# Nine transposed blocks instead of sixteen per attention tile, with new transfer costs in the planner of the first part

## The chip, the core and the metric

The kernel runs on one core of a Trainium2 chip. The metric is the device time of one execution in microseconds. Of the kernel before there are three timed runs (1258.95, 1251.04 and 1256.79 us, median 1256.79), and one execution with a profile.

## What is computed

Three layers follow each other. All matrices arrive in float32.

```python
# attention: 8 batches, 8 heads, 576 rows, 64 columns; keys and values are means over 8 neighbours: 72 per batch
k_p = k.reshape(B, H, Sp, pool, D).mean(axis=3)
v_p = v.reshape(B, H, Sp, pool, D).mean(axis=3)
attn = softmax(scale * q @ k_p.T)          # 576 x 72 for each head
x = attn @ v_p                             # put together to 4608 tokens x 512
# second layer, 512 -> 1024 -> 512
h = x @ w_in
ln = layernorm(h * softmax(h)) * g_ln
x = ln @ w_out
# third layer, 512 -> 2048 -> 512
h = x @ w2_in
out = (h * sigmoid(1.702 * h)) @ w2_out
```

## The kernel before, in words

Every fp32 factor is split into two fp16 parts, high and low, and a product is the sum of three fp16 products (high by high, high by low, low by high). The kernel has two parts. The **first part** computes the attention and the second layer in 36 tiles of 128 tokens, and meanwhile prepares the weights of the third layer: it joins the words of a float64 input, forms seven combinations of quarter matrices and writes their halves to DRAM. The **second part** (L1290 and the lines around it) computes the third layer in 12 blocks of 384 tokens by a Strassen-like scheme of seven products; its order is written out by hand and the change does not touch it.

In the first part a tile takes these steps. The scores go to `psx` (TensorE), the row maxima, exponentials and row sums give the normalized weights `e` (128 tokens x 8 heads x 72). ScalarE copies `e` to fp16 as the high half, VectorE or GpSimd subtracts to get the low half, and both go into `st`. A transposing DMA turns `st` into `aT`, in which the 72 keys lie on the partitions. TensorE multiplies `aT` with the transposed values `vst` into `psv`, ScalarE and VectorE split that into `xT`. Then `psh` holds x @ w_in, from which come the maximum `hmx`, the exponential `he`, the product `tt` with its sum, and the layer norm; `zs` is the fp16 split of its result, turned by another transposing DMA (16 blocks of 128x128) into `zT`. `psy` holds ln @ w_out; ScalarE copies it to `y`, and a DMA writes that to `y_dram`, from where the second part reads it. A transposed block is 128x128 fp16, which is 32 KB.

**The layout of the attention before.** A head has 256 columns in `st`: high (72), low (72), high again (72) and 40 zeros, so two blocks of 128 per head and 16 per tile. Values of a pair of heads have 256 columns in `vx` (high, high, low and 40 zeros), so eight blocks per batch in `vst`. A product of 216 used rows is so summed up by two matmuls over 128 partitions, each with 64 stationary columns (one head); the two heads of a pair write the upper and the lower 64 partitions of `psv`. Of the 36 tiles, 32 lie within one batch and four (4, 13, 22 and 31) in two, with 64 tokens of each; such a tile has twice the products, each over 64 columns.

**What sets the order.** The steps of all tiles, batches and weight chunks are generators (`attention`, `values`, `keys`, `Pair`, `Quarter`) that yield operations to a planner (`Plan`). It holds for each engine and for the DMA the time until which it is taken, picks the operation with the smallest start time (moved a little by due times), and emits it; each engine then runs its instructions strictly in that order. An operation that several engines could do (`VG`: VectorE or GpSimd) goes where it would end first. The cost of a transfer is written in `D` (L504 emits it): bytes over 360 per ns, and 1.23 times that if it transposes. All DMAs are issued by SyncE (SP) in one queue. The matmuls of the first part are emitted by `T` (L512), operations of the other engines by `op` (L475), so one line stands for many groups and the tiles' names tell them apart.

`vst` and `st` have two buffers each (by batch and by tile), `aT` two, `psv` and `psy` one, `y` two.

Of the kernel before, what the change touches and what calls it, by code (L numbers as in the profile page):

```python
# [18 lines left out]
P = 128  # L19
# [9 lines left out]
KM = DM // P  # L29
K1 = DF1 // P  # L30
K2 = DF2 // P
HS = 256
YB = 2 * P
TB = 384
TH = TB // 2
# [245 lines left out]
def moe_kernel(ctx: ExitStack, tc: tile.TileContext, qT, kT, vT, w_in, w_out, g_ln, w2_in, w2_out, eye, outT):  # L281
# [135 lines left out]
    with ExitStack() as ph:  # L417
# [9 lines left out]

        w1i = [wp.tile([P, KM, DF1], F16, name=f"w1i{i}") for i in range(2)]
        w1o = [wp.tile([P, K1, DM], F16, name=f"w1o{i}") for i in range(2)]
        vst = [wp.tile([P, H, P], F16, name=f"vst{i}") for i in range(2)]  # L430
        kbd = [wp.tile([P, NPAIR, 2 * SP], F32, name=f"kbd{i}") for i in range(2)]
        st = [wp.tile([P, H, HS], F16, name=f"st{i}") for i in range(2)]
        vx = kv.tile([P, NPAIR, 2 * P], F16, name="vx", bufs=1)

        plan = Plan()
        start, drop = plan.start, plan.drop
# [53 lines left out]
        def V(name, *args, **kw):  # L490
            return op(("dve",), name, args, kw)
# [4 lines left out]
        def VG(name, *args, **kw):  # L496
            return op(("pool", "dve"), name, args, kw)

        def A(**kw):
            return op(("act",), "activation", (), kw)  # L500

        def D(dst, src, turn=False, short=1):
            def emit(engine):
                (nc.sync.dma_start_transpose if turn else nc.sync.dma_start)(dst, src)  # L504

            n = math.prod(dst.shape) * mybir.dt.size(dst.dtype)
            return Op(("sp",), emit, [dst], [src], {"sp": n / 360 * (1.23 if turn else short)}, turn)

        def T(products):
            def emit(engine):  # L510
# [273 lines left out]
        def values(b, due):  # L784
            vp = yield from pooled("v", b, vT, due)
            am, alln, up, dn = s1("vam"), s1("v_all"), s1("v_up"), s1("v_dn")
            yield absmax_op(am, vp, axis=AX.XY)
            yield from largest(am, alln, TINY, b < 2)
            yield from power_scale("_v", alln, V_TOP, up, dn)
            yield lambda: b == 0 or v_ready[b - 1]  # L790
            yield A(
                out=vx[:, :, 0 : 2 * SP].rearrange("p a (r k) -> p a r k", r=2),
                in_=vp.unsqueeze(2).to_broadcast([P, NPAIR, 2, SP]), func=AF.Copy, scale=up,
            )
            yield V(
                "scalar_tensor_tensor", out=vx[:, :, 2 * SP : 3 * SP], in0=vp, scalar=up, in1=vx[:, :, 0:SP],
                op0=ALU.mult, op1=ALU.subtract,
            )
            drop(vp)
            yield lambda: b < 2 or valued[last_tile(b - 2)]  # L800
            yield D(vst[b % 2], vx.rearrange("p a k -> p (a k)"), turn=True)
            v_ready[b] = True
            yield w_in_done.over
            both = s1("v_sc", 2)
            c, ci = both[:, 0:1], both[:, 1:2]
            yield V("tensor_scalar", out=c, in0=dn, scalar1=1.0 / NPOOL, scalar2=w1i_dn, op0=ALU.mult, op1=ALU.mult)
            yield V("tensor_scalar", out=ci, in0=up, scalar1=w1i_up, scalar2=CI_LEAST, op0=ALU.mult, op1=ALU.max)
            yield V("tensor_scalar_min", ci, ci, CI_MOST)
            for t in range(NTILE):
                for o, n, tb in spans(t):  # L810
                    if tb == b:
                        yield G("tensor_copy", h_sc[o : o + n, t], both[o : o + n])
            h_ready[b] = True

        def attention(t):

            yield lambda: t == 0 or q_loaded[t - 1]
            qt = yield New(sb, [P, NPAIR, P], F32, "qt", bufs=2)
            q_loaded[t] = True
            yield D(qt, qT[t])  # L820
            if t < 2:
                tiles[t].due = max(due(t) + LAG_ATT, DUE_ATT + STEP_ATT * t)
            yield lambda: all(k_ready[b] for _, _, b in spans(t)) and (t == 0 or scored[t - 1])
            e = yield New(sb, [P, H, SP], F32, "e", bufs=2)
            yield there(qt, *(kbd[b % 2] for _, _, b in spans(t)))
            ps = yield New(psx, [P, 2, 512], F32, "psx", "psx")
            yield T(
                [
                    (
                        ps[o : o + n, p // 2, (p % 2) * 2 * SP : (p % 2 + 1) * 2 * SP],  # L830
                        qt[:, p, o : o + n],
                        kbd[b % 2][:, p, :],
                        True,
                        True,
                    )
                    for p in range(NPAIR)
                    for o, n, b in spans(t)
                ]
            )
            scored[t] = True  # L840
            drop(qt)
            s4 = ps[:, :, : 4 * SP].rearrange("p a (h k) -> p a h k", k=SP)
            mx = s1("mx", H)
            m3 = mx.rearrange("p (a h) -> p a h", a=2)
            yield V("tensor_reduce", out=m3, in_=s4, axis=AX.X, op=ALU.max, negate=True)
            if plan.free["act"] + ACT_SPARE < plan.free["dve"]:
                for h in range(H):
                    yield A(out=e[:, h], in_=s4[:, h // 4, h % 4], func=AF.Exp, bias=mx[:, h : h + 1])
                drop(ps)
            else:  # L850
                yield V(
                    "tensor_tensor", out=e.rearrange("p (a h) k -> p a h k", a=2), in0=s4,
                    in1=m3.unsqueeze(3).to_broadcast([P, 2, 4, SP]), op=ALU.add,
                )
                drop(ps)
                yield A(out=e, in_=e, func=AF.Exp)
            rs = s1("rs", H)
            yield V("tensor_reduce", out=rs, in_=e, axis=AX.X, op=ALU.add)
            yield A(out=rs, in_=rs, func=AF.Copy, scale=1.0 / A_TOP, bias=1e-9 / A_TOP)
            yield V("reciprocal", rs, rs)  # L860
            yield VG("tensor_tensor", out=e, in0=e, in1=rs.unsqueeze(2).to_broadcast([P, H, SP]), op=ALU.mult)
            yield lambda: t < 2 or turned[t - 2]
            s = st[t % 2]
            yield A(
                out=s[:, :, 0 : 3 * SP].rearrange("p h (r k) -> p h r k", r=3)[:, :, 0:3:2],
                in_=e.unsqueeze(2).to_broadcast([P, H, 2, SP]), func=AF.Copy,
            )
            yield VG("tensor_tensor", out=s[:, :, SP : 2 * SP], in0=e, in1=s[:, :, 0:SP], op=ALU.subtract)
            drop(e)
            aT = yield New(sb, [P, 2 * H, P], F16, "aT", bufs=2)  # L870
            yield D(aT, s.rearrange("p h c -> p (h c)"), turn=True)
            turned[t] = True
            yield lambda: all(v_ready[b] for _, _, b in spans(t)) and (t == 0 or valued[t - 1])
            yield there(aT, *(vst[b % 2] for _, _, b in spans(t)))
            ps = yield New(psv, [P, DM], F32, "psv", "psv")
            yield T(
                [
                    (
                        ps[h % 2 * D64 : (h % 2 + 1) * D64, h // 2 * P + o : h // 2 * P + o + n],
                        vst[b % 2][:, h // 2 * 2 + c, h % 2 * D64 : (h % 2 + 1) * D64],  # L880
                        aT[:, 2 * h + c, o : o + n],
                        c == 0,
                        c == 1,
                    )
                    for p in range(NPAIR)
                    for o, n, b in spans(t)
                    for c in range(2)
                    for h in (2 * p, 2 * p + 1)
                ]
            )  # L890
            valued[t] = True
            drop(aT)
            xT = yield New(sb, [P, 2 * KM, P], F16, "xT", bufs=2)
            turned_x = ps.rearrange("p (k t) -> p k t", t=P)
            yield A(out=xT[:, 0:KM], in_=turned_x, func=AF.Copy, scale=1.0 / A_TOP)
            yield V(
                "scalar_tensor_tensor", out=xT[:, KM:], in0=turned_x, scalar=1.0 / A_TOP, in1=xT[:, 0:KM],
                op0=ALU.mult, op1=ALU.subtract,
            )
            drop(ps)  # L900
            x_turned[t] = xT
# [269 lines left out]
        def clear(i, on):  # L1171
            if i == 0:
                yield G("memset", ones, 1.0)
                yield G("memset", minus_half, -0.5)
            yield on("memset", kbd[i], 0.0)
            yield on("memset", st[i], 0.0)
            if i == 0:
                yield G("memset", vx[:, :, 3 * SP :], 0.0)

        def eye_load():  # L1180
            yield D(eye_t, eye)
# [298 lines left out]
```

## Time and profile before

| | |
|---|---|
| median of three runs | 1256.79 us (1251.04 to 1258.95) |
| the profiled execution | 1253.29 us, of which the span from first to last instruction is 1251.5 us |
| TensorE busy | 1143.5 us, 91% |
| ScalarE, VectorE, GpSimd busy | 766.5, 730.9 and 664.7 us |
| DMA | 152.85 MB, of which the 16 engines moved most in the first 500 us |
| mean granted TensorE clock | 0.986 of full speed |

The first part ends at about 539 us, when the last product of `psy` is done; the second part takes the rest, with TensorE busy nearly throughout. A number such as 128x512 behind an operation is partitions by elements. The release named at an idle time ("<-DVE xT") is the event that came last before the instruction began.

### The profile page before, as it was taken

Reading aid. Unit: us, or ns where it says so; the run is one execution under the profiler, and the core shown is the slowest. Engines: PE = TensorE matmul, PEld = TensorE weight load, DVE = VectorE, ACT = ScalarE, POOL = GpSimd, SP = SyncE. Lnnn points to the kernel's source line nnn. Section 1 sums busy time; section 2 is a strip of 40 time slices with the busy share of each in tenths; the row PEclk is TensorE's granted clock in tenths of the full one; section 3 lists DMA queues with packets and bytes.
Section 4 is the critical chain, followed back from the end, with each engine's and each line's share of the span. In section 5 each row is a group of like instructions: output and inputs, shape, how many; then the busy total and the mean of one; then the engine's idle time right before and its main releaser. Section 6 shows DMA issues by size and latency. Waiting matters only on the chain.

```text
span 1251.5 us, 27586 instructions
## 1 busy us (share of the span) xinstructions
PE 1143.5 (91%) x11678; PEld 989.6 (79%) x11678; DVE 730.9 (58%) x1153; ACT 766.5 (61%) x1073; POOL 664.7 (53%) x696
## 2 busy tenths in 40 slices
PE   2778998899999999889999999999999999999998
PEld 2335665576666666789999999999999898999998
DVE  7898877587677843136455454637272737364543
ACT  6998998788789855345445353627263536454552
POOL 5887998687879953424333352525262515243331
PEclk9989999899999999999999999999999999999999
DMA  9979999999989698470101010100011010101000
GB/s 324 302 205 240 269 270 256 248 231 248 256 206 234 164 230 236 109 270 8 46 14 39 14 40 20 33 27 27 27 33 46 7 46 8 46 7 46 14 14 26
DMA packets 246524, 152.85 MB, mean 122 GB/s; under 512 B 163584, under 2 KB 226176, under 8 KB 244096
## 3 DMA queue, kind: packets, MB, share of 16 engines
q1 hardware_dynamic: 246400, 151.09, 45.5%
q8 instruction: 91, 1.49, 0.5%
q14 instruction: 33, 0.27, 0.1%
HBM read 77.66 MB, written 33.55 MB: 89 GB/s over the span
## 4 chain that ended last, share of the span: by engine, by line
PE 30%; POOL 12%; DVE 8%; ACT 8%; issue 5%; DMA 0%; ACTq 0%; POOLq 0%
PE bank_a L1290 18%; PE bank_d L1290 8%; ACT w_g L1325 6%; DVE g L1337 5%; POOL w_g L336 3%; PE bank_b L1290 3%; POOL w_g L335 3%; POOL w_g L333 2%; POOL w_g L334 2%; PE psy L512 2%; ACT g L1334 1%; DVE c L1303 1%; POOL zs L475 1%; DVE w_g L333 0%; ACT c L1300 0%
## 5 line engine op out<-in xcount | busy, mean ns | idle before, releaser
L1290 PEld LDWEIGHTS <-w2i 128*128 128x128 f16 x4032 | 337.4, 98 | 34.3 <-issue 33.7
L1290 PEld LDWEIGHTS <-w2o 128*128 128x128 f16 x4032 | 335.0, 98 | 7.4 <-issue 6.8
L333 POOL TENSOR_TENSOR w_g<-w_g 128x384 f32<-128x384 f32 x36 | 43.6, 1211 | 379.3 <-ACT w_g L1325 379.3
L1290 PE MATMUL bank_a<-ys,w2i 128*128 128x192 f16 x2304 | 215.1, 247 | 27.1 <-ACT c L1300 25.0
L512 PE MATMUL psh<-w1i,xT 128*128 128x512 f16 x864 | 205.8, 389 | 8.9 <-DVE mean L475 8.2
L1290 PE MATMUL bank_a<-g,w2o 128*128 128x192 f16 x2304 | 206.0, 246 | 1.0
L512 PE MATMUL psy<-zT,w1o 128*128 128x256 f16 x1728 | 196.8, 273 | 8.8 <-ACT y L475 8.8
L512 PEld LDWEIGHTS <-w1o 128*128 128x128 f16 x1728 | 167.9, 98 | 35.8 <-issue 10.3
L1337 DVE SCALAR_TENSOR_TENSOR g<-w_g,gu_b,g 128x1152 f16<-128x1152 f32 (+1 forms) x96 | 169.1, 1782 | 24.5 <-ACT g L1334 24.4
L512 PEld LDWEIGHTS <-xT 128*128 128x128 f16 x864 | 84.4, 100 | 103.9 <-issue 13.8
L1300 ACT ACTIVATE c<-bank_a 128x384 f32<-128x384 f32 x192 | 91.7, 484 | 116.4 <-PE bank_a L1290 113.1
L1334 ACT ACTIVATE g<-w_g,gu_b 128x1152 f16<-128x1152 f32 (+1 forms) x96 | 132.9, 1408 | 39.4 <-POOL w_g L336 39.0
L1303 DVE SCALAR_TENSOR_TENSOR c<-bank_d,c 128x384 f32<-128x384 f32 x96 | 53.3, 555 | 134.4 <-ACT c L1300 99.5
L475 POOL TENSOR_TENSOR zs<-tt,zs 128x1024 f16<-128x1024 f32 x36 | 77.4, 2149 | 59.7 <-ACT zs L475 59.5
L1290 PE MATMUL bank_d<-ys,w2i 128*128 128x192 f16 x1152 | 107.5, 249 | 0.3 <-DVE c L1303 0.3
L1290 PE MATMUL bank_d<-g,w2o 128*128 128x192 f16 x1152 | 102.4, 246 | 3.0 <-DVE g L1337 3.0
L1325 ACT ACTIVATE w_g<-c,ch_b 128x1536 f32<-128x1536 f32 x48 | 75.3, 1568 | 36.8 <-DVE c L1303 36.7
L1300 ACT ACTIVATE c<-bank_a,co_b 128x384 f32<-128x384 f32 x47 | 26.9, 573 | 108.6 <-PE bank_a L1290 108.6
L512 PE MATMUL psx<-kbd,qt 128*128 128x144 f32 (+1 forms) x320 | 46.3, 306 | 24.6 <-ACT raw_z L475 12.7
L512 PEld LDWEIGHTS psx<-kbd,qt 128*128 128x128 f32 (+1 forms) x320 | 41.4, 193 | 29.4 <-issue 12.7
L475 POOL TENSOR_TENSOR lo<-w_f,hi 128x512 f16<-128x512 f32 (+1 forms) x46 | 62.2, 1365 | 2.7 <-ACT hi L475 2.3
L475 DVE TENSOR_REDUCE hmx<-psh 128x1 f32<-128x1024 f32 x36 | 43.7, 1214 | 34.1 <-PE psh L512 34.1
(189 smaller groups left out, 1693.1 us busy)
## 6 DMA issues: line engine op xcount, KB each, us to landing
raw<-w_out SPq DMA_DIRECT2D x12, 1024.0 KB, 6.9
raw<-w_in SPq DMA_DIRECT2D x10, 1024.0 KB, 8.0
half<-kT SPq DMA_DIRECT2D x16, 576.0 KB, 5.4
half<-vT SPq DMA_DIRECT2D x16, 576.0 KB, 5.5
qt<-qT SPq DMA_DIRECT2D x36, 256.0 KB, 3.9
y_dram<-y SPq DMA_DIRECT2D x36, 256.0 KB, 2.8
y<-y_dram SPq DMA_DIRECT2D x48, 192.0 KB, 3.2
outT<-c SPq DMA_DIRECT2D x48, 192.0 KB, 1.9
```

The source lines that it names most:

```text
L333: eng.tensor_tensor(out=w[:, 1], in0=q[:, Q12], in1=q[:, Q11], op=ALU.subtract)
L334: eng.tensor_tensor(out=w[:, 2], in0=q[:, Q22], in1=w[:, 1], op=ALU.subtract)
L335: eng.tensor_tensor(out=w[:, 0], in0=q[:, Q22], in1=q[:, Q12], op=ALU.subtract)
L336: eng.tensor_tensor(out=w[:, 3], in0=q[:, Q21], in1=w[:, 2], op=ALU.subtract)
L475: getattr(eng, name)(*args, **kw)
L512: nc.tensor.matmul(*p[:3], start=p[3], stop=p[4])
L1290: nc.tensor.matmul(bank[:, q], self.weight(p, q, kk, w), self.data(p, kk, i), start=(first and q == 0 and kk == 0 and w == 0 and i == 0), ...
L1300: nc.scalar.activation(out=self.c[:, i], in_=bank, func=AF.Copy, scale=self.scale)
L1303: nc.vector.scalar_tensor_tensor(out=self.c[:, i], in0=bank, scalar=self.scale, in1=self.c[:, i], op0=ALU.mult, op1=ALU.add)
L1325: nc.scalar.activation(out=self.w[:, 0:4], in_=self.c, func=AF.Gelu_apprx_sigmoid, scale=self.ch)
L1334: nc.scalar.activation(out=self.g[:, 0, s], in_=self.w[:, s], func=AF.Copy, scale=self.gu)
L1337: nc.vector.scalar_tensor_tensor(out=self.g[:, 1, s], in0=self.w[:, s], scalar=self.gu, in1=self.g[:, 0, s], op0=ALU.mult, op1=ALU.subtract,)
```

## The change

The layout of the attention is packed tighter, and the planner's costs of transfers are changed.

- In `st` a head has one block of 128: its 72 high columns and the low columns of its first 56 keys. The low columns of the other 16 keys of all eight heads together are a ninth block. The second copy of the high half is gone, so ScalarE writes 576 elements per token and not 1152; the subtraction becomes two, of 8x56 and 8x16 elements.
- `vx` has three blocks per pair of heads (12 per batch, not 8): high values of all keys and again of the first 56, low values of the 72 keys, and high values of the last 16 keys of both heads for the ninth block. ScalarE writes it in four operations and not one.
- A pair of heads now takes five products per part of a tile: two over the first block and two over the second, each with 64 stationary columns, as before, and one over the ninth block with 128 stationary columns for both heads.
- The zeros in `st` are no longer needed, so its two memsets go; `vx` is cleared once as a whole.
- The planner's cost of a transfer is now bytes over 330 per ns, and over 170 if it transposes (before: 360, and 360/1.23 = 293). All of its decisions from then on may differ.

```diff
+LEFT = 2 * SP - P
...
-        vst = [wp.tile([P, H, P], F16, name=f"vst{i}") for i in range(2)]
+        vst = [wp.tile([P, 3 * NPAIR, P], F16, name=f"vst{i}") for i in range(2)]
...
-        st = [wp.tile([P, H, HS], F16, name=f"st{i}") for i in range(2)]
-        vx = kv.tile([P, NPAIR, 2 * P], F16, name="vx", bufs=1)
+        st = [wp.tile([P, H + 1, P], F16, name=f"st{i}") for i in range(2)]
+        vx = kv.tile([P, NPAIR * (3 * P + 2 * LEFT)], F16, name="vx", bufs=1)
+        vx3 = vx[:, 0 : 3 * NPAIR * P].rearrange("p (g k) -> p g k", k=P)
...
-            return Op(("sp",), emit, [dst], [src], {"sp": n / 360 * (1.23 if turn else short)}, turn)
+            return Op(("sp",), emit, [dst], [src], {"sp": n / (170 if turn else 330)}, turn)
...
-            yield A(
-                out=vx[:, :, 0 : 2 * SP].rearrange("p a (r k) -> p a r k", r=2),
-                in_=vp.unsqueeze(2).to_broadcast([P, NPAIR, 2, SP]), func=AF.Copy, scale=up,
+            even, odd = vx3[:, 0::3], vx3[:, 1::3]
+            yield A(out=even[:, :, 0:SP], in_=vp, func=AF.Copy, scale=up)
+            yield V(
+                "scalar_tensor_tensor", out=odd[:, :, 0:SP], in0=vp, scalar=up, in1=even[:, :, 0:SP], op0=ALU.mult,
+                op1=ALU.subtract,
             )
...
+            yield A(out=even[:, :, SP:P], in_=vp[:, :, 0 : P - SP], func=AF.Copy, scale=up)
+            for j in range(2):
+                r = slice(j * D64, (j + 1) * D64)
+                yield A(
+                    out=vx[r].rearrange("p (a x) -> p a x", a=NPAIR)[:, :, 2 * P + j * LEFT : 2 * P + (j + 1) * LEFT],
+                    in_=vp[r, :, P - SP :], func=AF.Copy, scale=up[r],
+                )
...
+        def of_pair(out, p, at, aT, vst):
...
+            heads = [(slice(j * D64, (j + 1) * D64), 2 * p + j) for j in range(2)]
+            return [
+                *((out[r], vst[:, 3 * p, r], aT[:, h, at], True, False) for r, h in heads),
+                *((out[r], vst[:, 3 * p + 1, r], aT[:, h, at], False, False) for r, h in heads),
+                (out, vst[:, 3 * p + 2], aT[:, H, at], False, True),
+            ]
...
-            yield A(
-                out=s[:, :, 0 : 3 * SP].rearrange("p h (r k) -> p h r k", r=3)[:, :, 0:3:2],
-                in_=e.unsqueeze(2).to_broadcast([P, H, 2, SP]), func=AF.Copy,
+            first, rest = slice(0, P - SP), slice(P - SP, SP)
+            yield A(out=s[:, 0:H, 0:SP], in_=e, func=AF.Copy)
+            yield VG("tensor_tensor", out=s[:, 0:H, SP:P], in0=e[:, :, first], in1=s[:, 0:H, first], op=ALU.subtract)
+            yield VG(
+                "tensor_tensor", out=s[:, H].rearrange("p (h k) -> p h k", k=LEFT), in0=e[:, :, rest],
+                in1=s[:, 0:H, rest], op=ALU.subtract,
             )
-            yield VG("tensor_tensor", out=s[:, :, SP : 2 * SP], in0=e, in1=s[:, :, 0:SP], op=ALU.subtract)
...
-            aT = yield New(sb, [P, 2 * H, P], F16, "aT", bufs=2)
+            aT = yield New(sb, [P, H + 1, P], F16, "aT", bufs=2)
...
-            yield on("memset", st[i], 0.0)
             if i == 0:
-                yield G("memset", vx[:, :, 3 * SP :], 0.0)
+                yield G("memset", vx, 0.0)
```

TensorE's queue gains the fifth product of each pair and part of a tile, 160 in all (640 products into `psv` become 800): 128 of them over 128 moving columns, 32 (of the four tiles that lie in two batches) over 64.

The first place where rows move is ScalarE's queue at the values of batch 5. Before, `vx` is written by one instruction (`vp` are the pooled values, `v_up` their scale):

```order
L475 ACTIVATE diag_3696<-eye_t_87,vam_3266 128x128
L475 ACTIVATE tt_3411<-tt_3411,mean_2769,a_3442 128x1024
L475 ACTIVATE raw_2494<-raw_2494,w2o_up_77 128x512
L475 ACTIVATE vx_125<-vp_3037,v_up_3268 128x4x144
L475 ACTIVATE zs_3715<-tt_3411 128x1024
L475 ACTIVATE raw_2494<-raw_2494,w2o_up_77 128x512
```

With the change the four pieces have other work between them:

```order
L478 ACTIVATE tt_3241<-tt_3241,mean_2855,a_3584 128x1024
L478 ACTIVATE vx_125<-vp_3182,v_up_3447 128x4x72
L478 ACTIVATE zs_3826<-tt_3241 128x1024
L478 ACTIVATE vx_125<-vp_3182,v_up_3447 128x4x56
L478 ACTIVATE diag_3807<-eye_t_87,w2a1_144 128x128
L478 ACTIVATE vx_125<-vp_3182,v_up_3447 64x4x16 x2
```

The last write of `vx`, on which the transpose into `vst` waits, now stands behind a `zs` and a `diag` that lie between the pieces.

The second place is SP's queue at the key halves of batch 6 (`half<-kT`; tile 27 is the first that needs them). Before, both are issued behind the transposes `aT` of the first 20 tiles:

```order
L504 DMA y_dram1_64<-y_2830 128x2x256
L504 DMA_TRANSPOSE aT_2860<-st1_124 128x16x128
L504 DMA w2i_dram_69<-hi_2707 128x7x256
L504 DMA half_2946<-kT 128x1152
L504 DMA half_2947<-kT 128x1152
L504 DMA w2i_dram_69<-lo_2723 128x7x256
L504 DMA y_dram1_64<-y_2938 128x2x256
```

With the change the two stand behind the transposes of 25 tiles, apart from each other:

```order
L507 DMA_TRANSPOSE zT_3813<-zs_3826 128x16x128
L507 DMA_TRANSPOSE aT_4013<-st0_123 128x9x128
L507 DMA half_3387<-kT 128x1152
L507 DMA_TRANSPOSE zT_3813<-zs_3957 128x16x128
L507 DMA y_dram2_65<-y_3934 128x2x256
L507 DMA half_3881<-vT 128x1152
L507 DMA half_3414<-kT 128x1152
```

The key halves moved from seven tiles ahead of their use to two.

The third place is SP's queue near the end of the first part, where the weights of the second part (`w2i`) and its first tokens (`y_6097`, in the change `y_6429`) are loaded. Before:

```order
L504 DMA w2i3_5791<-w2i_dram_69 128x4096
L504 DMA_TRANSPOSE zT_6014<-zs_6016 128x16x128
L504 DMA w2i6_5794<-w2i_dram_69 128x4096
L504 DMA y_6097<-y_dram0_63 128x2x192
L504 DMA_TRANSPOSE zT_6014<-zs_6056 128x16x128
L504 DMA y_6097<-y_dram0_63 128x2x192 x3
L504 DMA y_dram4_67<-y_6135 128x2x256
L504 DMA y_dram4_67<-y_6212 128x2x256
```

And with the change:

```order
L507 DMA_TRANSPOSE zT_6245<-zs_6278 128x16x128
L507 DMA y_dram4_67<-y_6351 128x2x256
L507 DMA w2i3_6039<-w2i_dram_69 128x4096
L507 DMA w2i6_6042<-w2i_dram_69 128x4096
L507 DMA y_dram4_67<-y_6424 128x2x256
L507 DMA y_6429<-y_dram0_63 128x2x192 x3
L507 DMA_TRANSPOSE zT_6453<-zs_6455 128x16x128
```

One write of `y` now goes out ahead of the last two weight loads, and the next one ahead of the token loads.

## Rows read from the trace of the kernel before

**Rows 1.** Stretches: length, PE, PEld, DVE, ACT, POOL busy, clock, DMA share, GB/s.

```profile
36.00:95.00 59.00, 43.81 (x295) 21.97 (x294) 51.80 (x101) 54.07 (x93) 49.18 (x55) 0.88 0.90 250
95.00:450.00 355.00, 328.50 (x2638) 226.32 (x2635) 268.05 (x498) 303.37 (x479) 303.15 (x380) 0.99 0.98 235
450.00:540.00 90.00, 80.38 (x652) 61.86 (x651) 21.97 (x39) 38.96 (x50) 30.44 (x47) 1.00 0.69 188
540.00:1251.00 711.00, 680.17 (x8053) 669.81 (x8050) 360.00 (x466) 343.58 (x406) 260.86 (x188) 0.99 0.11 37
```

**Rows 2.** DMA of 95 to 450 us: queue share; issues, times, us to landing.

```profile
q1 hardware_dynamic: 171209, 83.04, 97.6%
...
aT<-st SPq DMA_TRANSPOSE x29, 4.2
zT<-zs SPq DMA_TRANSPOSE x28, 5.1
vst<-vx SPq DMA_TRANSPOSE x6, 3.4
```

**Rows 3.** Two short stretches, columns as above.

```profile
475.00:480.00 5.00, 5.00 (x29) 2.74 (x28) 3.15 (x7) 4.00 (x5) 1.86 (x2) 1.00 1.01 388
500.00:505.00 5.00, 1.98 (x19) 1.62 (x17) 1.39 (x3) 3.34 (x6) 4.60 (x8) 1.00 0.93 210
```

**Rows 4.** PE's waits, 0 to 95 us: us in total, times, longest.

```profile
PE psv L512 <- DMA aT<-st: 12.9, 4, 7.3
```

**Rows 5.** PE's waits, 95 to 500 us.

```profile
PE psv L512 <- DVE xT L475: 10.3, 5, 5.2
...
PE psv L512 <- DMA vst<-vx: 3.5, 2, 1.8
```

**Rows 6.** DVE's waits, 95 to 500 us.

```profile
DVE w2am L475 <- DMA raw<-w_out: 13.2, 4, 5.6
```

**Rows 7.** Timeline around 242 us, DVE and PE: start, us, operation, [idle before].

```profile
242.67 1.35 DVE L475 TENSOR_REDUCE kp<-half 128x144 f32<-128x1152 f32 x1 [5.77 <-DMA half<-kT]
...
245.81 0.80 PE L512 MATMUL psv<-diag,ones 128*128 128x128 f32 x2 [5.21 <-DVE xT L475]
246.40 4.50 PE L512 MATMUL psh<-w1i,xT 128*128 128x512 f16 x12
```

**Rows 8.** Timeline of PE, three groups of products in a row.

```profile
112.08 2.78 PE L512 MATMUL psy<-zT,w1o 128*128 128x256 f16 x24
114.80 0.64 PE L512 MATMUL psv<-aT,vst 128*64 128x128 f16 x16
115.37 2.79 PE L512 MATMUL psy<-zT,w1o 128*128 128x256 f16 x24
```

**Rows 9.** Groups by line: xcount, busy us, mean ns, idle before.

```profile
L512 PEld LDWEIGHTS <-w1o 128*128 128x128 f16 x1728 | 167.9, 98 | 35.8 <-issue 10.3
```

**Rows 10.** Groups of the other engines, 0 to 520 us.

```profile
L475 POOL TENSOR_TENSOR w_f<-w_f 128x256 f32<-128x256 f32 x61 | 45.9, 764 | 1.7 <-DVE w_f L475 1.0
L475 POOL TENSOR_TENSOR st<-e,st 128x576 f16<-128x576 f32 x34 | 44.7, 1315 | 10.5 <-ACT st L475 6.4 <-issue 3.6
...
L475 ACT ACTIVATE st<-e 128x1152 f16<-128x1152 f32 x36 | 41.5, 1156 | 12.2 <-POOL e L475 6.8 <-DVE e L475 5.3
...
L475 ACT ACTIVATE e<-e 128x576 f32<-128x576 f32 x36 | 24.2, 672 | 2.0 <-DVE e L475 2.0
```

**Rows 11.** Timeline near the end of the first part: SP, then ACT.

```profile
482.31 5.89 SPq L504 DMA_TRANSPOSE zT<-zs  x1
488.25 1.61 SPq L504 DMA_DIRECT2D y<-y_dram  x3
489.95 5.19 SPq L504 DMA_DIRECT2D y_dram<-y  x2
...
494.16 0.60 ACT L475 ACTIVATE y<-psy 128x512 f32<-128x512 f32 x1 [8.77 <-DMA y_dram<-y]
```

**Rows 12.** PE's waits, 500 to 545 us.

```profile
PE psy L512 <- ACT y L475: 5.3, 3, 3.0
```

More of the change, by code (lines that the diff above doesn't have):

```diff
@@ L31 @@
 K2 = DF2 // P
-HS = 256
+LEFT = 2 * SP - P
 YB = 2 * P
@@ L500, in A, with D @@
             return op(("act",), "activation", (), kw)
-        def D(dst, src, turn=False, short=1):
+        def D(dst, src, turn=False):
             def emit(engine):
@@ L790, in values @@
             yield lambda: b == 0 or v_ready[b - 1]
-            yield A(
-                out=vx[:, :, 0 : 2 * SP].rearrange("p a (r k) -> p a r k", r=2),
-                in_=vp.unsqueeze(2).to_broadcast([P, NPAIR, 2, SP]), func=AF.Copy, scale=up,
-            )
[L795 to L798, printed above, removed]
+            even, odd = vx3[:, 0::3], vx3[:, 1::3]
[3 more added lines that the diff above has]
+                op1=ALU.subtract,
+            )
+            yield A(out=even[:, :, SP:P], in_=vp[:, :, 0 : P - SP], func=AF.Copy, scale=up)
[5 more added lines that the diff above has]
+                )
             drop(vp)
             yield lambda: b < 2 or valued[last_tile(b - 2)]
-            yield D(vst[b % 2], vx.rearrange("p a k -> p (a k)"), turn=True)
+            yield D(vst[b % 2], vx[:, 0 : 3 * NPAIR * P], turn=True)
             v_ready[b] = True
@@ L877, in attention @@
                 [
[L878 to L884, printed above, removed]
+                    x
                     for p in range(NPAIR)
                     for o, n, b in spans(t)
-                    for c in range(2)
-                    for h in (2 * p, 2 * p + 1)
+                    for x in of_pair(ps[:, p * P + o : p * P + o + n], p, slice(o, o + n), aT, vst[b % 2])
                 ]
```

## The prediction

> **What bounds the kernel now.** I read the stretches first, because the shares of the whole span mix two parts with different limits. Each row of [rows 1] is a stretch with the busy time of each engine, the granted clock and the DMA's share. The reader is to see three things. From 540 us on TensorE is busy 680 of 711 us, the DMA 0.11: the second part is TensorE's, and nothing of the change lies there. From 95 to 450 us TensorE is busy 328.5 of 355 us (93%) and the DMA 0.98 of the time: two resources are nearly full at once, and TensorE's idle time of 26.5 us is the most that this stretch could give back if the work stayed as it is. From 36 to 95 us TensorE is idle 15 of 59 us at a mean clock of 0.88, while ScalarE (54) and VectorE (52) are nearly full. The tail, 450 to 540 us, has 9.6 us of idle TensorE.
>
> Next come the waits, which say what TensorE's idle time hangs on: in the first 95 us 12.9 us in four waits for `aT` [rows 4]; from 95 to 500 us 10.3 us for `xT` of VectorE and 3.5 us for `vst` [rows 5]. VectorE in turn waits for loads (13.2 us for the raw weights alone [rows 6]). The timeline shows how such a wait reaches TensorE: VectorE stands 5.77 us before `kp`, since the key halves are not there; `xT`, which is queued behind it, comes late; TensorE stands 5.21 us and then needs 4.50 us for twelve products of `psh` [rows 7], which is 375 ns for 512 columns, where two products of 256 columns in a row take 2 x 113 ns (24 in the 2.72 us from 112.08 to 114.80 [rows 8]). That is its lower clock level after the pause.
>
> **The change, part by part.** The sum is made against the profiled execution's own 1253.3 us, which is 3.5 us under the median of the three runs and inside their spread.
>
> *Products (+8.3).* 128 more over 128 columns and 32 over 64. The trace has no fp16 product of 128 stationary and 128 moving columns. From below: 113 ns for 256 columns, so 57 for 128 and 28 for 64 [rows 8], in all 8.2 us. From above: a load of 128 weight columns takes 98 ns [rows 9]; if none of it were hidden, 160 x 98 = 15.7 us. I take the row that is nearest in shape: 16 half-width products of `psv` last from 114.80 to 115.37, so a pair of them, which fills the array's width once, takes 71 ns [rows 8]; 128 x 71 + 32 x 36 = 10.3 us. 29 of 36 tiles lie behind 95 us [rows 2], where TensorE is nearly full: 8.3 us on the path (6.6 to 12.6). The other seven tiles lie in the stretch with 15 us of idle time and cost nothing unless that goes.
>
> The Trainium skill (TensorE: Matmul & The Clock Gate, section Back-to-back issue gap) gives about 81 ns for a product of 128 columns in a sustained stream with weight loads, and only 56 for one by itself; by it, as an estimate, the products would cost some 11.7 us and not 10.3, and the sum would be a little over 1 us higher. No row here shows such a stream.
>
> *Transposed blocks.* In the stretch 95 to 450 us, `aT` has 29 x 16 blocks, `zT` 28 x 16 and `vst` 6 x 8: 960 blocks of 32 KB, or 31.5 of the 83.0 MB [rows 2]. The cheapest price is that of two `zT` nearly alone: 0.93 of 5 us for 1.05 MB, 0.145 us per block, or 226 GB/s [rows 3]. The dearest comes from the whole stretch: plain loads at 388 GB/s and share 1.01 [rows 3] would need 134 us for the other 51.6 MB; 346 us are used, which leaves 212 us for 960 blocks, 0.22 each. The change takes away 29 x 7 blocks and adds 6 x 4: 179 fewer, so 26 to 39 us of 346, and the DMA's share falls to some 0.88. This is not a term of the sum: it pays only through waits.
>
> The Trainium skill (Advanced Engine Details and Errata, section X-Bar Transpose (TRN2)) says that transposes run as fast as plain transfers, at 350 to 400 GB/s. The trace disagrees: 226 GB/s in the stretch where little else runs [rows 3]. By the page the blocks would save only about 15 to 17 us (an estimate), the planner's new price would be false, and the next two gains would be about half of what I take.
>
> *Waits of the first 95 us (-4).* A transposition of nine blocks is shorter by seven, 1.0 to 1.5 us; four waits [rows 4] give 4 to 6 us. I take the low end, because the chain before it (GpSimd's subtraction) gets no shorter. Bounds: 0, and the whole 12.9.
>
> *VectorE's waits for loads (-9).* The stall of [rows 7] costs 5.2 us and about 1.8 us by the lower clock (4.50 against 12 x 0.226 = 2.7). Its key halves were issued and read early; in the new order they are issued five tiles later, alone, and VectorE's read is moved back too. With the DMA no longer full I take that 7.0 as gone, and 2 of the other 5.1 us of waits for `xT` [rows 5]. Late next is `hmx`, which waits for TensorE and so costs nothing. Bounds: the whole 10.3 + 1.8, and a new wait of the same size (+7), as the halves now have two tiles to spare and not seven.
>
> *The values at a change of batch (+5).* `vst` gets 12 blocks for 8: 0.6 to 0.9 us longer. ScalarE writes `vx` in four pieces: two rows give it 0.84 ns per element and 188 ns fixed (1152 in 1156 ns, 576 in 672 [rows 10]), so 0.43 + 0.38 + 2 x 0.24 = 1.29 us where one instruction of 576 elements took about 0.67; and between the pieces stand a `zs` (1024 elements, about 1.05 us) and a `diag` (0.30). `vst` comes some 2.5 us later than now, six times behind 95 us. Two of these were waited for already [rows 5]: 2 x 2.5 = 5. Bounds: 0 where products of other tiles cover it, 15 if all six are bare.
>
> *The tail (-4).* ScalarE's `y` stood 8.77 us for the write of an earlier `y`, which was issued only at 489.95, behind a `zT` and three token loads [rows 11]; behind it on ScalarE are the next `zs`, and TensorE then waited 5.3 us for `y` [rows 12]. The new order issues these writes ahead of the last weight loads and the token loads. I take 4 of the 5.3. Bounds: 0, -9.6.
>
> *Off the path.* ScalarE saves 36 x 0.48 = 17 us on `st` and gives back 8 x 0.6 on `vx`; it is busy 303 of 355 us and does not end the waits. GpSimd has two subtractions (448 and 128 elements) for one of 576: by 1315 and 764 ns for 576 and 256 elements [rows 10] one more fixed part of about 0.32 us, 31 times, 10 us in all. TensorE covers it while GpSimd is at 303 of 355 us [rows 1]; without that cover it would cost the share behind 95 us, 8 us. The memsets at the start go or shrink; TensorE has no work then, and VectorE's is under 1 us.
>
> Sum: 8.3 - 4 - 9 + 5 - 4 = -3.7, so 1249.6 us. **I forecast 1250 us**, no change by measure. A change of under 1% (12.6 us: under 1244.2 or over 1269.4 against the median) can't be told from none here.
>
> **The rivals.**
> - *The forecast*, gains and costs nearly cancel: 1243 to 1257, chance 0.42; a third of it lies under 1244.2.
> - *The DMA was the bound*, and TensorE's idle time falls to 2% of the stretch: (328.5 + 8.3) / 0.98 = 344 for 355, -11; with the head and the tail, 1234. For it: share 0.98, and VectorE's waits for loads. Against: the second part, with the DMA at 0.11, still has TensorE idle for 4% [rows 1], and at that the stretch would need 352. Chance 0.18.
> - *The freed DMA time buys nothing*: the waits stay and only change places, since the order is another one throughout; then +8.3 for the products and up to +5 for the values, 1258 to 1267. This is also the case that the new prices don't do what they say: at 170 GB/s the planner holds back transfers that by [rows 3] can run at 226. Chance 0.26.
> - *Slower*: the full-width product cannot overlap its weight load with the half-width ones around it, and each costs the 98 ns of [rows 9], 12.6 us behind 95 us; with the values' 5 and no gain this is 1271, and more with bare batch changes. It decides from about 85 ns per product on, narrow ones too (160 x 0.085 x 29/36 = 11, and 5, so +16 against the profiled execution). For it: TensorE is 93% full where they come. Against: `psv` took 71 ns per pair with two loads in it. The skill's 81 ns lies just under that point. Chance 0.14.
>
> **The numbers.** Faster: 0.18 + 0.14 = 0.32. Slower: 0.14 and a rest of the third case, 0.15. Within 1%: 0.53. The range leaves out the deep end of the second case and the slower one: 1232 to 1268.
>
> **What will show it.** Products: the gap from one group's start to the next around 20 products of `psv`; 0.85 us (0.57 + 4 x 0.071) if right, 0.96 if at 98 ns. Blocks: the DMA's share over the same stretch at 0.86 to 0.90. Waits: PE's waits for `aT` in the first 95 us near 9, none of 5 us behind `kp`, `vst` waits near 8, `y` waits after 500 us under 2. I am wrong if the last `psy` ends before 525 or after 552 us, for the second part should last its 711 us in any case.

## The result: 1% slower, by a product that I priced more than three times too low

The change takes 1267.03 us (median of 8 runs, 1263.54 to 1272.15), the kernel before 1257.55 us over as many runs. The ratio is 1.0104 (95% interval 1.0081 to 1.0127), 9.5 us by the medians. The range ended at 1268, so the time lies inside it; the direction and the forecast of 1250 are wrong. The profiled execution of the change is the slowest of its runs, 1272.15 us with a span of 1270.4; that of the kernel before (1253.29) lies under its median. The two traces are so 18.9 us apart, twice the 9.5 us of the medians, and lengths taken from them overstate the loss.

The stretches of the profile after, as in [rows 1] (length; PE, PEld, DVE, ACT, POOL busy; clock; DMA share; GB/s):

```profile
36.00:95.00 59.00, 46.31 (x295) 24.39 (x294) 49.30 (x96) 50.24 (x93) 49.46 (x60) 0.94 0.78 223
95.00:450.00 355.00, 342.33 (x2619) 231.07 (x2621) 266.45 (x488) 282.45 (x483) 289.89 (x383) 0.97 0.87 212
...
557.00:1270.00 713.00, 681.07 (x8062) 670.79 (x8061) 361.74 (x467) 343.90 (x407) 261.09 (x188) 0.99 0.11 37
```

The last products of `psy`, before and after (timelines of PE: start, us, operation, number):

```profile
530.25 5.40 PE L512 MATMUL psy<-zT,w1o 128*128 128x256 f16 x48 [0.73 <-ACT y L475]
...
548.83 5.40 PE L515 MATMUL psy<-zT,w1o 128*128 128x256 f16 x48 [0.19 <-ACT y L478]
```

They end at 535.7 and 554.2 us, the latter past the 552 that I had named as a sign of being wrong. Then follows a wait of 3.4 us in both, and the second part lasts 713 us as before (711). The DMA share fell from 0.98 to 0.87, as forecast (0.86 to 0.90). TensorE is busier than before, 342 of 355 us for 328.5, and yet the stretch contains fewer products of `psy` and `psh` (1152 and 612 for 1228 and 642), since the first part lasts longer. So TensorE was not kept waiting; it had more to do. The granted clock of the stretch is 0.97 for 0.99. The timeline of PE around one group of `psv` (start, us, operation, number):

```profile
453.61 2.78 PE L515 MATMUL psy<-zT,w1o 128*128 128x256 f16 x24
456.32 1.65 PE L515 MATMUL psv<-aT,vst 128*64 128x128 f16 x20
457.80 2.78 PE L515 MATMUL psy<-zT,w1o 128*128 128x256 f16 x24
```

From the start of the group to the start of the next it is 1.48 us (1.49 in most others); before, it was 0.57 for 16 products [rows 8]. I had named 0.85 as right and 0.96 as the sign of the slower rival; it is neither. A tile that lies in two batches takes 2.44 us (443.43 to 445.87) for 0.62 before (419.65 to 420.27). Over the first part that is 32 x 0.92 + 4 x 1.82 = 36.7 us more work for TensorE, where I had 10.3.

The waits of PE, as in [rows 4, 5, 12] (us in total, times, longest), first 0 to 95, then 95 to 500, then 500 to 570 us:

```profile
PE psv L515 <- DMA aT<-st: 1.9, 2, 1.5
...
PE psv L515 <- DVE xT L478: 1.7, 2, 1.3
...
PE psy L515 <- DMA zT<-zs: 2.6, 2, 2.0
PE psy L515 <- ACT y L478: 1.3, 2, 1.1
```

`aT` is waited for 1.9 us and not 12.9, `xT` 1.7 and not 10.3, `y` 1.3 and not 5.3; `vst` is not in the list. The forecast signs of a gain are there, and the kernel is slower.

### The profile page after: what moved, and what is told of

It is laid out like the page before. It is cut to its first block, busy times and chain, and to the rows that moved or that the text cites. A ratio compares the mean times of both kernels' runs of the same rounds, so it can differ in the third digit from the quotient of the medians.

```text
span 1270.4 us, 27958 instructions
## 1 busy us (share of the span) xinstructions
PE 1183.9 (93%) x11838; PEld 1010.2 (80%) x11838; DVE 739.3 (58%) x1154; ACT 757.4 (60%) x1104; POOL 673.5 (53%) x728
## 4 chain that ended last, share of the span: by engine, by line
PE 54%; POOL 15%; DVE 13%; ACT 10%; issue 5%; DMA 3%; SPq 0%; ACTq 0%; DVEq 0%; POOLq 0%
PE bank_a L1302 18%; PE psh L515 11%; PE psy L515 10%; PE bank_d L1302 8%; ACT w_g L1337 6%; DVE g L1349 5%; PE psv L515 4%; POOL w_g L336 3%; POOL w_g L335 3%; PE bank_b L1302 2%; POOL w_g L333 2%; POOL w_g L334 2%; PE psx L515 2%; POOL w_f L478 1%; ACT g L1346 1%
## 5 line engine op out<-in xcount | busy, mean ns | idle before, releaser
L515 PE MATMUL psh<-w1i,xT 128*128 128x512 f16 x864 | 209.3, 393 | 10.3 <-DVE mean L478 4.0
L515 PEld LDWEIGHTS <-vst 128*64 128x64 f16 (+1 forms) x800 | 39.2, 107 | 40.2 <-issue 16.7
L515 PE MATMUL psv<-aT,vst 128*64 128x128 f16 (+3 forms) x800 | 65.5, 232 | 5.4 <-DMA aT<-st 3.0
```

Source lines behind the costliest of these rows:

```text
L515: nc.tensor.matmul(*p[:3], start=p[3], stop=p[4])
```

## Experiments

Each kernel ran interleaved with the kernel before, whose median was 1254.4 to 1256.0 us in these runs.

**1 and 2. Which products cost the time.** Both keep the change's order on every engine and alter only the products of `psv`: e1_halves does the wide one (128 stationary columns) as two of 64, e2_grouped puts all 64-column products of a tile (the first four of each pair) ahead of its four wide ones.

```diff
 e1_halves, in of_pair
-                (out, vst[:, 3 * p + 2], aT[:, H, at], False, True),
+                *((out[r], vst[:, 3 * p + 2, r], aT[:, H, at], False, True) for r, h in heads),
```

> The ninth block's product is done as two products with 64 stationary columns (one head each) and not as one with 128; the order of every engine is otherwise that of the change. Theory (each change between 64 and 128 stationary columns on TensorE costs time: in the trace of the change a pair of heads takes 0.37 us where two pairs of half-width products took 0.142): a pair now takes 3 x 0.071 = 0.21 us, a tile's group 0.85 us and not 1.49, TensorE has some 26 us less work, and the time falls to 1241 to 1252 us. Rival 1 (a third set of products per pair is dear in itself, by its number): the group stays at 1.2 us or more, 1260 or more. Rival 2 (the new order of the planner made it slower, and TensorE's products lie beside other waits): 1262 to 1272 whatever the group takes.

```diff
 e2_grouped, in attention
-            yield T(
...
+            products = [
+                x
+                for part in (slice(0, 4), slice(4, 5))
+                for p in range(NPAIR)
+                for o, n, b in spans(t)
+                for x in of_pair(ps[:, p * P + o : p * P + o + n], p, slice(o, o + n), aT, vst[b % 2])[part]
+            ]
+            yield T([(*x[:3], i < 2, i == len(products) - 1) for i, x in enumerate(products)])
```

> The same products as in the change, but within a tile all 64-column ones come first and the four 128-column ones last, so that a tile has two changes of width and not eight. Theory (the change of width costs): a group takes about 0.57 + 4 x 0.057 + one or two changes of 0.09 = 0.9 to 1.0 us and not 1.49; 1244 to 1254 us. Rival 1 (a 128-column product over 128 moving columns takes 0.23 us by itself, as its weight load is not hidden): the group stays at 1.4 to 1.5 us and the time at 1264 to 1271. Rival 2 (the order): 1262 to 1272 whatever the group takes.

e1_halves: 1247.14 us, ratio 0.993 (0.9901 to 0.9958). e2_grouped: 1246.22 us, 0.9926 (0.9905 to 0.9947). The timelines of PE, first e1_halves:

```profile
454.49 0.86 PE L515 MATMUL psv<-aT,vst 128*64 128x128 f16 x24
455.28 2.79 PE L515 MATMUL psy<-zT,w1o 128*128 128x256 f16 x24
```

and e2_grouped, the last line from the timeline of the weight loads (PEld):

```profile
455.82 0.97 PE L515 MATMUL psv<-aT,vst 128*64 128x128 f16 x20
456.63 2.78 PE L515 MATMUL psy<-zT,w1o 128*128 128x256 f16 x24
...
456.57 0.10 PEld L515 LDWEIGHTS <-w1o 128*128 128x128 f16 x1
```

The load of the next weights, those of `psy`, starts 0.06 us ahead of its product, while wide products of `psv` still run. 24 half-width products take 0.79 us, and the very products of the change, sorted by width, 0.81 us. So a product with 128 stationary columns costs (0.81 - 0.57) / 4 = 60 ns, near the 57 of my lower bound and under the 81 ns that I had quoted from the Trainium skill (TensorE: Matmul & The Clock Gate, Back-to-back issue gap). Both times hold one change of width, away from the half-width products. It is the change of width between neighbours that costs: rival 1 of each expectation falls by its own run, rival 2 by both. Sorting also moves a wide product away from the half-width ones that sum into the same columns of `psv`; e7 tells the two apart. The time fell by 20 us where I had expected 13 to 26.

**7. The mix of widths in the old kernel.** To see it without nine blocks and without a new order, the kernel before got one more product of 128 stationary columns per pair and part of a tile, times a tile of zeros (`zero`); the planner does not count it, so the order stays. The line that adds it:

```diff
+                ] + [(ps[:, p * P + o : p * P + o + n], vst[b % 2][:, 2 * p], zero[:, o : o + n], False, True)]
```

> The kernel before, its order and its 16 blocks, with one more product per pair and part of a tile: 128 stationary columns of vst times a tile of zeros, added to the same psv, so that the values do not change. It puts the change's mix of widths into the old kernel and nothing else. Theory (width changes cost): a tile's group takes about 1.5 us and not 0.57, TensorE has 37 us more work, of which waits cover a part: 1270 to 1292 us. Rival (a product of 128 columns is worth 57 to 71 ns, and the change's loss lies in its order or in the ninth block's wait): 1257 to 1266 us.

1272.54 us, ratio 1.0133 (1.0111 to 1.0155). Here the two widths carry different names, so the timeline separates them (last line: PEld):

```profile
117.61 0.30 PE L513 MATMUL psv<-aT,vst 128*64 128x128 f16 x4
117.84 0.23 PE L513 MATMUL psv<-zero,vst 128*128 128x128 f16 x1
118.00 0.30 PE L513 MATMUL psv<-aT,vst 128*64 128x128 f16 x4
...
117.84 0.10 PEld L513 LDWEIGHTS <-vst 128*128 128x128 f16 x1
```

Four half-width products (0.14 us at the old pace) hold the next wide one off until 0.23 us after their start, so 0.09 us is lost on the way to full width; the wide one starts 0.16 us before the next half-width one, of which 0.06 is its own, so about as much is lost on the way back. That next one belongs to another pair and sums into other columns, so a shared sum can't be the reason there. The load (last line) says more: the weights of the wide product are not loaded while half-width ones run, but start together with it at 117.84, where between products of one width a load starts ahead (0.06 us in e2). Why the load waits is not shown. The row of PE's stretch tells what becomes of it:

```profile
95.00:450.00 355.00, 343.88 (x2650) 231.58 (x2649) 252.34 (x484) 292.65 (x463) 291.05 (x366) 0.98 0.95 229
```

Some 37 us more work made the kernel 16.5 us slower, within the 1270 to 1292 expected. The rest went into waits that TensorE had anyway: its idle time here is 11 us for 26.5 in [rows 1], with the order unchanged and the DMA still at 0.95. The shorter waits of the change are therefore no proof that transfers land earlier; a slower TensorE waits less.

**6. What the fewer blocks are worth.** As e1_halves, order untouched, but each `aT` is transposed with 16 blocks, seven of them never read (cleared once at the start), while the planner counts nine (`counted`).

```diff
-        st = [wp.tile([P, H + 1, P], F16, name=f"st{i}") for i in range(2)]
+        st = [wp.tile([P, 2 * H, P], F16, name=f"st{i}") for i in range(2)]
...
-            aT = yield New(sb, [P, H + 1, P], F16, "aT", bufs=2)
-            yield D(aT, s.rearrange("p h c -> p (h c)"), turn=True)
+            aT = yield New(sb, [P, 2 * H, P], F16, "aT", bufs=2)
+            yield D(aT, s.rearrange("p h c -> p (h c)"), turn=True, counted=H + 1)
```

> As e1_halves, with the same order on every engine and the planner counting nine blocks, but each transpose into aT moves 16 blocks again (the last seven hold zeros and are never read). If the fewer transposed blocks are what pays for e1_halves (8 us under the kernel before), the DMA's share from 95 to 450 us is back at 0.97 or more, TensorE's waits for aT, xT and VectorE grow again, and the time is 1253 to 1262 us. Rival (the blocks' time was hidden anyway, and only the other order or ScalarE's shorter copy gains): 1243 to 1250 us.

1248.37 us, ratio 0.9935 (0.9912 to 0.9957), against 0.993 for e1_halves. The DMA has the share of before the change (its stretch of 95 to 450 us):

```profile
95.00:450.00 355.00, 336.38 (x2893) 233.94 (x2892) 269.79 (x504) 292.89 (x500) 305.58 (x396) 0.99 0.98 236
```

and in e1_halves it is not:

```profile
95.00:450.00 355.00, 340.36 (x2938) 237.72 (x2933) 273.82 (x506) 296.31 (x506) 311.04 (x408) 0.99 0.89 223
```

0.98 or 0.89, the time is the same within the intervals. In this order the transposes' time was hidden, and the rival of this run holds.

**3, 4 and 5. Layout and prices apart.** e3_old_costs and e5_halves_old_costs have the new layout (with the change's products, and with half-width ones) and the planner's old prices; e4_new_costs has the old layout and the new prices.

```diff
 e3, e5
-            return Op(("sp",), emit, [dst], [src], {"sp": n / (170 if turn else 330)}, turn)
+            return Op(("sp",), emit, [dst], [src], {"sp": n / 360 * (1.23 if turn else 1)}, turn)
 e4 (kernel before)
-            return Op(("sp",), emit, [dst], [src], {"sp": n / 360 * (1.23 if turn else short)}, turn)
+            return Op(("sp",), emit, [dst], [src], {"sp": n / (170 if turn else 330)}, turn)
```

> The layout of the change with the planner's old transfer costs (bytes over 360, times 1.23 if transposing). Theory (the products cost the time, the new costs help or do nothing): 1263 to 1280 us, no faster than the change. Rival 2 (the new costs made the order worse): under 1258.

> The layout of the kernel before, 16 blocks per tile, with the planner's new transfer costs alone. Theory: the waits for transfers shrink by the better order, 1243 to 1257 us. Rival 2 (the new costs made the order worse): 1264 or more.

> Nine blocks with half-width products only, and the planner's old transfer costs. With the change's own products the new costs made 1270.5 to 1267.0 us, with the old layout 1255.4 to 1266.3. Theory (the products were the loss; which costs suit is left to the order that comes out): 1241 to 1257 us, within 1% of the 1247 us with new costs. Rival (the new costs are what gains now): 1257 or more.

e3: 1270.54 us, 1.0126 (1.0092 to 1.016): the products' loss is there with the old prices too, 15 us against e5. e4: 1266.28 us, 1.0084 (1.0056 to 1.0111): my theory expected 1243 to 1257 and missed, and its rival (1264 or more) holds. e5: 1255.34 us, 0.9998 (0.998 to 1.0017), inside 1241 to 1257: nine blocks without mixed widths and without new prices are worth nothing. With new prices the same layout is 8 us faster (e1), the old one 11 us slower (e4). In e4 the waits of PE from 95 to 560 us say where:

```profile
PE psh L512 <- DVE mean L475: 15.3, 7, 5.6
PE psy L512 <- ACT y L475: 9.2, 6, 2.7
PE psh L512 <- DVE nm L475: 6.5, 2, 3.4
```

TensorE stands before products of `psh` whose accumulators VectorE has not yet read (`mean` and `nm` come from an earlier `psh`). No transfer is among the three, which points at the order of the engines' work. That the order is the whole of the 11 us is not shown: the granted clock from 95 to 450 us is 0.97 in this trace and 0.99 before.

**8 to 12. Are the prices better, or only other?** e8, e9 and e10 are e1_halves with other prices, e11 and e12 the kernel before with other prices; the edit is the line above.

> As e1_halves, with the planner's costs at the rates that the short stretches of the trace before showed, bytes over 226 per ns for transposes and over 340 for the rest. If costs nearer to the undisturbed rate give a better order: 1236 to 1244 us. If the costs are no more than another draw of the order: 1240 to 1258 us, without a rule.

> As e1_halves, the transposing price a little lower: bytes over 180 per ns for 170. If the gain of e1_halves over e5_halves_old_costs (8 us) comes from prices near the trace's rates, a step of 6% between 170 (1247 us) and 226 (1244 us) must lie there too: 1242 to 1249 us. If every price is only another draw of the order, it may lie anywhere from 1242 to 1262, and a value over 1250 shows it.

> As e1_halves, bytes over 160 per ns for transposes. Prices near the trace's rates as the cause: 1244 to 1251 us, as 0.20 us per block lies inside the bounds that the trace gave (0.145 to 0.22). Another draw: anywhere from 1242 to 1262, over 1252 shows it.

> The kernel before with 16 blocks and the planner's prices at 226 and 340 bytes per ns, which gave the fastest order with half-width nine blocks (1244 us). If these prices are better for their own sake: 1243 to 1251 us here too, against 1255 for its own prices. If the order is a draw that depends on the layout as well: 1252 to 1270.

> The kernel before with 16 blocks and prices of 180 (transposing) and 330, a step of 6% from e4_new_costs (170 and 330: 1266 us, 11 slower than with its own prices, while 226 and 340 made it 12 faster). If 170 was one bad draw of the order: 1242 to 1257 us. If dear transposes suit 16 blocks badly, as the planner then holds back too much: 1259 to 1270.

| bytes per ns, transposing / plain | nine blocks, half-width products | 16 blocks (kernel before) |
|---|---|---|
| 293 / 360 (old) | 1255.34, ratio 0.9998 | 1254.4 to 1256.0, by definition 1 |
| 226 / 340 | 1244.19, 0.9907 (0.9884 to 0.993) | 1241.88, 0.989 (0.9869 to 0.9911) |
| 180 / 330 | 1246.10, 0.9923 (0.9904 to 0.9942) | 1249.83, 0.9964 (0.9949 to 0.9979) |
| 170 / 330 (new) | 1247.14, 0.993 (0.9901 to 0.9958) | 1266.28, 1.0084 (1.0056 to 1.0111) |
| 160 / 330 | 1249.78, 0.9962 (0.9943 to 0.9982) | |

e9 and e10 lie where better prices were expected (another draw could fall there as well), e12 where one bad draw at 170 was; e8, just above one of its ranges and inside the other, decides nothing; e11 is just under the range of its theory. With nine blocks neighbouring prices from 226 to 160 give times within each other's intervals, rising from 1244 to 1250 us. With 16 blocks the step from 180 to 170 costs 16 us, so one order can be a bad draw. 226 / 340 has the lowest time in both columns, though with nine blocks it can't be told from 180 / 330, and at this price the tighter layout gains nothing either (0.9907 against 0.989). That a price is better for being nearer to a measured rate is not shown: 226 takes a DMA share of 1 for the most, but while a `zT` moves alone the trace before has a share of 1.27 and 289 GB/s, next to the old price of 293 (501 to 502 us, columns as in [rows 3]):

```profile
501.00:502.00 1.00, 0.33 (x4) 0.15 (x2) 0.94 (x1) 0.00 (x0) 1.00 (x2) 1.00 1.27 289
```

e11_old_226, the old layout with one line changed, has the lowest time of all kernels: 13 us under the kernel before and 25 under the change. Its stretch of 95 to 450 us:

```profile
95.00:450.00 355.00, 334.89 (x2689) 229.54 (x2688) 272.75 (x501) 305.75 (x482) 309.88 (x391) 1.00 1.01 239
```

The DMA is at 1.01, fuller than in any other run here, and the time is the lowest.

## Why the prediction was wrong, step by step

- **Products (+8.3).** This is the step that failed, as a size. The measured sum is 36.7 us in the first part; in the trace of the change 27 whole tiles and three in two batches lie behind 95 us, 27 x 0.92 + 3 x 1.82 = 30.3 us. My two bounds, 57 and 98 ns, were prices of a product or a load among its like; the place of the new one, between products of another width, was in neither. The slower rival named the right place (the wide product beside half-width ones), and its reason, that the load does not overlap them, is what e7 shows. But it was priced at one load, 98 ns, where as much is lost at the change back and a wide product costs 0.23 us (1.48 - 0.57 over four); I gave it a chance of 0.14. The 71 ns that I took had a change of width in them too: in e1 eight more half-width products, four pairs, lengthen the group by 0.22 us, 55 ns a pair. The trace before had a trace of it: 24 products of `psy` ahead of a `psv` group take 2.72 us from start to next start (112.08 to 114.80), the 24 behind it 2.63 (115.37 to 118.00), which is 0.09 us for one change of width. I took the first as the pace of `psy` and read past the difference. The line behind them:

```profile
118.00 1.15 PE L512 MATMUL psx<-kbd,qt 128*128 128x144 f32 x8
```

- **Waits of the first 95 us (-4), VectorE's waits (-9).** The named waits shrank more than forecast, but not for the reason I gave. For `xT` e7 has 3.6 us instead of 10.3 with no new order and hardly less DMA: a busier TensorE absorbs them. For `aT` e7 still has 9.1 of 12.9 us, and e6, with 16 blocks in the new order, 4.3, so most of the fall there comes with the order and not with shorter transposes. Other waits took its place: all of TensorE's waits in the first 95 us sum to 33.9 us for 40.6, and its idle time from 36 to 95 us is 12.7 for 15.2. e6 has the old DMA share and loses nothing. The share of 0.98 was read as half a bound; it was none, and 1.0 is not its top: it is 1.27 while a `zT` moves alone (501 to 502 us, above). What moved time was the order: 8 us for the change's prices with half-width products (e5 to e1).
- **Transposed blocks (no term).** The share fell as forecast. But I read 226 GB/s as the rate of a transpose, and it is 289: my 0.145 us per block is a price in share, and 32 KB at 289 GB/s take 0.113 us.
- **Values at a change of batch (+5).** No wait for `vst` from 95 to 500 us in the trace of the change. That is my lower bound; that products of other tiles covered the later `vst` was not traced.
- **The tail (-4).** The wait for `y` fell from 5.3 to 1.3 us, as forecast, but waits for `zT` (2.6 us) came in; 1.4 us net.
- **Off the path.** ScalarE and GpSimd stay at 282 and 290 of 355 us; no run tests them alone.
- **The whole.** 36.7 us of work, less about 20 that waits absorb (e7: 37 us in, 16.5 out), less 8 for the order, is +9; measured is +9.5. This sum takes pieces from different kernels and is a check of size, not a proof that they add up. The third rival, that the freed DMA time buys nothing, ends at 1267 us, where the time came out (its own terms give 1262 to 1267, not 1258). That is luck: it had the products at 8.3 us and the waits staying, and neither was so. The time's place just inside my range is luck as well.

Open stays why 170 / 330 gives a bad order with 16 blocks and not with nine. e12 shows that the loss is not there yet at 180, but which decision of the planner tips was not traced.

## What to carry to other kernels

A new instruction is priced by its neighbours, not by its shape alone: look in the trace for the same kind of change between neighbours, and put products of one width together (or split the wide one) before spending anything else. A resource that is 98% busy is a bound only if someone waits for it; add the load back in one run, as in e6, before paying for its removal. Where a planner sets the order, a cost model's figure is a tuning knob whose effect is measured for each layout, since a step of 6% here moved the time by 16 us.

## What the runs showed of the hardware

- Between matmuls with 64 and with 128 stationary columns TensorE loses about 0.1 us each way (e7), and the weights of the new width are loaded only as its first product starts (117.84 in e7); the wide product itself costs 60 ns over 128 moving columns (e2).
- A DMA share of 0.98 did not slow this kernel: 0.98 and 0.89 gave 1248.4 and 1247.1 us (e6, e1). The share can pass 1: it was 1.27 at 289 GB/s while one transpose moved alone (before, 501 to 502 us).
